# A many-part edit of a two-layer SSM-convolution and MLP training step, with some elementwise products moved to GpSimd

## The chip, the cores and the metric

The kernel runs on one core of a Trainium2 chip. The metric is device time in microseconds: the median of three runs. One further execution was recorded by the hardware profiler, and all rows below come from that one. Engines are named as in the profile: PE is TensorE's matmul, PEld its weight load, DVE is VectorE, ACT is ScalarE, POOL is GpSimd and SP is SyncE. DMAs can be issued from the queues of SP, ACT and POOL.

## The reference

The program is a forward pass of four residual blocks and its full backward pass. Block A is an H3-like layer with a long convolution; block B is an MLP. S is 2048, D is 448, F is 1792, everything in bf16.

```python
def _A_ref(q, k, v, shift_k, ssm_k, ssm_D):
    ...
    for t in range(ks):
        k_shift = k_shift + k_pad[:, t:t + S, :] * shift_k[:, ks - 1 - t][None, None, :]
    kv = k_shift * v
    ...
    y_f = kv_f * kf_f[None, :, :, :]
    y = irfft2(y_f)[:, 0, :S, :]
    y = y + kv * ssm_D[None, None, :]
    return q * y

def _B_ref(x, w1, w2):
    h = _silu(jnp.einsum("bsd,df->bsf", x, w1))
    return jnp.einsum("bsf,fd->bsd", h, w2)

x = A_q
x = x + _A_ref(_layernorm(x, axis=-1), A_k, A_v, A_shift_k, A_ssm_k, A_ssm_D)
x = x + _B_ref(_layernorm(x, axis=-1), B_w1, B_w2)
x = x + _A_ref(_layernorm(x, axis=-1), A_k, A_v, A_shift_k, A_ssm_k, A_ssm_D)
x = x + _B_ref(_layernorm(x, axis=-1), B_w1, B_w2)
return x
```

The outputs are x and the gradients of all inputs but `B_x`. The convolution's result y does not depend on x, so it is computed once and used in both A blocks.

## The kernel before, in words

There are three stages.

**Prefix** (`_ssm_prefix`, 0 to 101 us). The long convolution is done by a two-step Fourier transform on TensorE. For the filter k: its rows are loaded and transposed (L337), a first transform of 16 parts n2 (`_fft_stage1`, L203: two matmuls into a PSUM tile, one copy of 128x896 to SBUF by `_copy`), a turn by seven times 16 transposes (`turn`, L349), and a second transform in 14 blocks of 1024 columns (`_fft_stage2`, L211). `cons_ka` (L397) copies each block of k's spectrum into `Ka`, stores every two blocks to DRAM (`SPEC_d["K"]`, L404), and `_swap_halves_dma` (L241) writes a copy `KB` in which partitions 0 to 63 and 64 to 127 have changed places. All of these DMAs are issued by GpSimd. In the same loop the short convolution of k and the product with v are made (`conv`, L365), and `stage1_kv` (L384) does the first transform of kv, with a copy of 128x448 for each part. `KB` shares its memory with the transposed k and the filter's first rows, so the swaps of blocks 0 to 7 stand after the last convolution (L419). After that loop come the loads of w1 (SP), of the first quarter of grad_out (`gb0`) and of A_q (`x0c0`), both from GpSimd, and the first layernorm of `x0c0` (`_ln`, L253: statistics on VectorE, a power on GpSimd at L270, normalisation on VectorE, a store to `N_d`). Then kv is turned and transformed, and `cons_prod` (L445) does for each of the 14 blocks: copy the block out of PSUM, store kv's spectrum every two blocks, and on VectorE multiply it with `Ka` (L456, `pa`) and with `KB` (L457, `pb`). The inverse transform of a block (`_fft_inv_stage2_chunk`, L222) runs on TensorE two blocks later. The result y goes into `Ysb`.

Copies out of PSUM are given to ScalarE or VectorE by `_Bal` (L87): a running sum of estimated time for each, to which the code adds other work by hand (`bal.add`).

**Main** (`Main.run`, L769, 101 to 510 us). Four chunks of 512 rows go through both layers forward and back. TensorE's order is written out by hand: `H`, `O`, `G`, `N` and `T` are generators of the products with w1, w2, w2 transposed, w1 transposed, and of transposes, and a pattern string gives the order of their steps (`weave`, `steps`). The other engines take their instructions in the order that the scheduler makes of the program. `fwd0(c)` makes the first two layernorms of a chunk and its gate with y, `fwd1(c)` those of the second layer. `O` adds its PSUM result to `X` on VectorE (L685), and in layer 1 stores the finished chunk of `X` to out_0 (L687) when its fourth tile is done. `N` for layer 1 writes the gradient G1 over the same rows of `X` (`Gt`, L723 and `_ln_bwd`, L899). `Main.__init__` stores `Ysb` to `Y_d` from GpSimd (L536).

**Weight gradients and suffix** (`Jobs`, `_ssm_suffix`, 440 us to the end). `Jobs` multiplies stored operands, loaded by SP (L963) as stationary blocks `dstat`, into the gradients of w1 and w2; `fin_w2` (L1051) copies a finished part and stores it from GpSimd. `_ssm_suffix` is the backward pass of the convolution, with the stored spectra loaded by `spec_load` (L1146) and the inverse transform's matrix by `_load_minv` (L199, 1 MB), both from GpSimd. TensorE alternates between the two.

Of the kernel before, what the change touches and what calls it, by code (L numbers as in the profile page):

```python
# [13 lines left out]
ALU = mybir.AluOpType  # L14
# [3 lines left out]
P = 128  # L18
# [184 lines left out]
def _fft_stage1(k, n2, rhs, A1, psum, m=None):  # L203
    nc = k.nc
    ps = psum.tile([P, 2, 512], FP32, name="ps_s1", **k.pt["s1"])
    for c in range(2):
        nc.tensor.matmul(ps[:, c, :D], lhsT=k.M1sb[:, n2 if m is None else m, c, :], rhs=rhs, start=True, stop=True)
    _copy(nc, k.bal.pick(2 * D) if m is None else nc.scalar, A1[:, :, :, n2, :].rearrange("p dh c ds -> p c dh ds"), ps[:, :, :D].rearrange("p c (dh ds) -> p c dh ds", ds=4))
# [44 lines left out]
def _ln(k, pool, c, src, si, n_g, groups=((0, 4),), pin=False, eng=None, behind=None):  # L253
    nc = k.nc
    for lo, hi in groups:
# [3 lines left out]
        for tl in range(lo, hi):  # L259
# [6 lines left out]
            nc.vector.bn_aggr(out=mv[:, tl, :], in_=st[:, tl, :])  # L266
        ve = pool.tile([P, 4], FP32, name="ln_ve", tag="ln_ve", bufs=2)
        nc.vector.tensor_scalar(out=ve[:, 0:n], in0=mv[:, lo:hi, 1], scalar1=EPS, scalar2=None, op0=ALU.add)  # L268
        r = k.rstd[si][:, 4 * c:4 * c + 4]
        nc.gpsimd.tensor_tensor(out=r[:, lo:hi], in0=ve[:, 0:n], in1=k.mhalf[:, 0:n], op=ALU.pow)  # L270
# [7 lines left out]
    if si != 2:  # L278
        lo, hi = groups[0][0], groups[-1][1]
        nc.gpsimd.dma_start(out=_pm(k.N_d[si][:])[:, 4 * c + lo:4 * c + hi, :], in_=n_g[:, lo:hi, :])  # L280


def _ssm_prefix(k):
# [4 lines left out]
    with ExitStack() as es:  # L288
# [35 lines left out]
        for h in range(2):  # L324
            nc.sync.dma_start(out=vn[:, 8 * h:8 * h + 8, :], in_=v_pm[:, 8 * h:8 * h + 8, :])
        _load_minv(k, nc.sync)
        nc.sync.dma_start_transpose(out=k.w2T[:, 0:3, :], in_=k.B_w2[:, 0:384])
        nc.sync.dma_start_transpose(out=k.w2T[:, 3:4, :], in_=k.B_w2[:, 320:448])
# [16 lines left out]
        for n2 in (*range(1, 16), 0):  # L345
            _fft_stage1(k, n2, Kt[:, n2, :], A1K, psum)
# [37 lines left out]
        def stage1_kv(h, jq, kvt):  # L384
            for u in range(0, 4, 2):
# [5 lines left out]
                for w in range(2):  # L391
                    _copy(nc, bal.pick(2 * DH), A1kv[:, 56 * h:56 * (h + 1), :, n2 + w, :].rearrange("p dh c ds -> p c dh ds"),
                          ps[:, w, :, :DH].rearrange("p c (dh ds) -> p c dh ds", ds=4))
# [3 lines left out]
        def cons_ka(ci, ps):  # L397
            sl = slice(ci * 1024, (ci + 1) * 1024)
            _copy(nc, bal.pick(1024), Ka[:, sl], ps[:])
            if ci % 2 == 1:  # L400
                lo, hi = (ci - 1) * 1024, (ci + 1) * 1024
                if ci > 8:
                    _swap_halves_dma(k, KB, Ka, lo, hi, nc.gpsimd)
                nc.gpsimd.dma_start(out=k.SPEC_d["K"][:, lo:hi], in_=Ka[:, lo:hi])  # L404

        prev = None
        for h in range(2):
            for i, jq in enumerate((1, 2, 3, 0)):
# [8 lines left out]
                else:  # L417
                    _fft_stage2(k, Z, psum, cons_ka, range(2 * i, 2 * i + 2))
        for i in range(4):  # L419
            _swap_halves_dma(k, KB, Ka, 2048 * i, 2048 * (i + 1), nc.gpsimd)  # L420
# [8 lines left out]
        k.gb0 = _hd(k, [P, 4, D], "gb0")  # L429
        nc.gpsimd.dma_start(out=k.gb0[:], in_=_pm(k.grad_out[0])[:, 0:4, :])  # L430
        k.x0c0 = _hd(k, [P, 4, D], "x0c0")
        nc.gpsimd.dma_start(out=k.x0c0[:], in_=_pm(k.A_q[0])[:, 0:4, :])
        k.na0 = _hd(k, [P, 4, D], "na0")
        _ln(k, work, 0, lambda tl: k.x0c0[:, tl, :], 0, k.na0, pin=True)


# [8 lines left out]
        def cons_prod(ci, ps):  # L445
# [11 lines left out]
            nc.vector.tensor_tensor(out=pb[:], in0=xs, in1=KB[:, sl], op=ALU.mult)  # L457
            bal.add("dve", 1.4)
# [65 lines left out]
class Main:  # L524
    def __init__(self, k, es):
# [10 lines left out]
        nc.gpsimd.dma_start(out=_pm(k.Y_d[:]), in_=k.Ysb[:])  # L536
# [61 lines left out]
    def a_fwd(self, c, si, src, n_g, groups, behind=None):  # L598
        nc, X = self.nc, self.X
        if len(groups) > 2:  # L600

            for g in groups:
                _ln(self.k, self.ch, c, src, si, n_g, (g,))
                self.gate(c, src, n_g, (g,))
            return
# [18 lines left out]
    def fwd0(self, c):  # L624
# [14 lines left out]
        n01 = self.t([P, 4, D], "n01", bufs=2)  # L639
        _ln(k, self.ch, c, self.xs(c), 1, n01)  # L640
        self.n0[c] = (n00, n01)

    def fwd1(self, c, behind=None):
        n10, n11 = self.t([P, 4, D], "n10"), self.t([P, 4, D], "n11")
        pairs = ((0, 2), (2, 4)) if c else ((0, 2), (2, 3), (3, 4))
        self.a_fwd(c, 2, self.xs(c), n10, pairs, behind)
        _ln(self.k, self.ch, c, self.xs(c), 3, n11, pairs)
# [28 lines left out]
    def O(self, c, L, aT):  # L676
        nc, k, X = self.nc, self.k, self.X
        for tl in range(4):
# [7 lines left out]
            if L == 1 and tl == 3:  # L686
                nc.gpsimd.dma_start(out=_pm(k.outs[0][0])[:, 4 * c:4 * c + 4, :], in_=X[:, 4 * c:4 * c + 4, :])  # L687
# [26 lines left out]
    def N(self, c, L, gh, gres, n_b, n_a):  # L714
# [4 lines left out]
        for tl in range(4):  # L719
# [3 lines left out]
            Gt = self.X[:, t, :] if L == 1 else g1[:, tl % 2, :]  # L723
            pn = k.psum.tile([P, 512], FP32, name="ps_n", tag="po", bufs=2)
# [6 lines left out]
            _ln_bwd(k, self.ch, u0[:], n_b[:, tl, :], cp[:, tl, :], gres(tl), Gt)  # L731
            if L == 1:
                nc.vector.tensor_tensor(out=gyt[:, tl, :], in0=Gt, in1=n_a[:, tl, :], op=ALU.mult)
                u1 = self.t([P, D], "lb_u1", "lb_u0", 3)
                nc.vector.scalar_tensor_tensor(out=u1[:], in0=Gt, scalar=k.rstd[2][:, t:t + 1], in1=self.Y[:, t, :], op0=ALU.mult, op1=ALU.mult, accum_out=cp[:, 4 + tl, 0:1])
                self.chain = _ln_bwd(k, self.ch, u1[:], n_a[:, tl, :], cp[:, 4 + tl, :], Gt, Gt)
# [32 lines left out]
    def run(self, es):  # L769
# [19 lines left out]
        with tc.high_priority():  # L789
            self.fwd0(0)  # L790
        nT = self.nT()
# [7 lines left out]
        steps("GGGtttt", G=g20, t=self.T2(self.n0[0][1], nT))  # L799
# [20 lines left out]
        for c in range(4):  # L820
# [6 lines left out]
            o = self.O(c, 1, aT2)  # L827
            if c == 0:
                weave("O" * 8, O=o)
            else:  # L830
# [5 lines left out]
                if c == 1:  # L836
                    weave("OOOOOGGOGGOTOT", O=o, G=g, T=self.T(self.n0[c + 1][1], nT))
# [492 lines left out]
```

## Time and profile before

| | us |
|---|---|
| median of 3 runs (725.36 to 734.2) | 729.11 |
| the profiled execution | 729.0 |
| its span, first to last instruction | 727.2 |
| TensorE matmul busy | 685.5 (94%) |
| VectorE busy | 489.0 (67%) |
| ScalarE busy | 444.3 (61%) |
| GpSimd busy | 126.4 (17%) |

The span is what the rows below can explain; 1.8 us lie around it. Busy shares are means over stages with different limits. A matmul's recorded time holds its pipeline, so TensorE can look busy where it is fed slowly. In the groups and the timeline a row reads: line, engine, operation, output and inputs, shapes, count; the bracket at its end gives the idle time of that engine just before the row and what ended it. The granted clock is the share of full clock that TensorE was given. Rows of the timeline that are merged have a count above one.

### The profile page before, as it was taken

What the parts mean: (1) busy time and instruction counts of PE and PEld (TensorE: products, weight loads), DVE (VectorE), ACT (ScalarE), POOL (GpSimd) and SP (SyncE); (2) the same over time, 40 slices, a digit from 0 to 9 for tenths busy, and PEclk for the clock granted to TensorE, in tenths of its full rate; (3) what the DMA queues carried; (4) which work ended last, traced back from release to release, by engine and by line L of the source; (5) the groups of instructions that cost most, each with busy time, mean ns of one, the idle gap of its engine ahead of it and who ended that gap; (6) DMA issues with size and microseconds to landing.
All of it is one profiled execution on the core that took longest, in us unless ns stands there. A gap on an engine that the chain in (4) does not pass through costs nothing.

```text
span 727.2 us, 12726 instructions
## 1 busy us (share of the span) xinstructions
PE 685.5 (94%) x4933; PEld 377.5 (52%) x4976; DVE 489.0 (67%) x1157; ACT 444.3 (61%) x585; POOL 126.4 (17%) x213
## 2 busy tenths in 40 slices
PE   5997889998989999999999999999899999999996
PEld 4986644434444444444444444545466666656553
DVE  4789865656897747976379534825168768859760
ACT  4887877686777868779687783132755555454200
POOL 1134410201011100111001000000312323244220
PEclk9999999999999999999999999999999999999999
DMA  9949799899989999499985997199998798789860
GB/s 315 292 141 289 249 298 135 126 264 248 211 202 243 220 240 242 109 228 262 186 200 130 244 244 299 30 222 218 369 411 298 251 337 288 244 307 357 314 210 20
DMA packets 195581, 172.59 MB, mean 237 GB/s; under 512 B 142882, under 2 KB 173730, under 8 KB 194368
## 3 DMA queue, kind: packets, MB, share of 16 engines
q1 hardware_dynamic: 180992, 115.73, 63.1%
q0 software_dynamic: 14064, 56.04, 22.2%
q8 instruction: 39, 0.64, 0.4%
q14 instruction: 22, 0.18, 0.1%
q10 hardware_dynamic: 464, 0.00, 0.0%
HBM read 73.25 MB, written 60.10 MB: 183 GB/s over the span
## 4 chain that ended last, share of the span: by engine, by line
PE 59%; issue 10%; DVE 6%; DMA 3%; ACT 3%; POOL 2%; SPq 1%; POOLq 0%; DVEq 0%
PE ps_d L969 12%; PE ps_g L499 10%; PE ps_n L726 10%; PE ps_h L499 9%; PE ps_o L681 8%; PE ps_d L1004 2%; DMA dstat<-a_d 2%; PE ps_v L228 2%; PE ps_v L227 2%; PE ps_t L567 1%; DMA out_dram<-X 1%; DVE B1v L1276 1%; PE ps_tr L1158 1%; ACT dT L674 1%; DVE gka L1277 1%
## 5 line engine op out<-in xcount | busy, mean ns | idle before, releaser
L969 PEld LDWEIGHTS <-dstat 128*128 128x128 bf16 x800 | 75.5, 98 | 69.0 <-DMA dstat<-a_d 4.0
L499 PE MATMUL ps_h<-nT,w1sb 128*128 128x512 bf16 (+1 forms) x434 | 95.9, 380 | 5.6 <-ACT dT L664 2.2
L681 PE MATMUL ps_o<-w2sb,aT 128*128 128x448 bf16 x448 | 88.8, 352 | 4.0 <-DVE X L685 4.0
L726 PE MATMUL ps_n<-w1T,ghT 128*128 128x448 bf16 x448 | 92.1, 352 | 0.1
L499 PE MATMUL ps_g<-nT,w2T 128*128 128x512 bf16 (+1 forms) x378 | 81.1, 380 | 1.1 <-issue 0.5
L709 ACT CAST ghT<-ps_g 128x512 bf16<-128x512 f32 (+1 forms) x74 | 54.1, 761 | 42.4 <-PE ps_g L499 42.2
L659 ACT ACTIVATE aT<-ps_h 128x512 bf16<-128x512 f32 (+1 forms) x82 | 59.9, 758 | 29.9 <-PE ps_h L499 27.4
L499 PEld LDWEIGHTS <-w1sb 128*128 128x128 bf16 (+1 forms) x448 | 35.5, 97 | 61.7 <-issue 27.7
L681 PEld LDWEIGHTS <-aT 128*128 128x128 bf16 x448 | 43.5, 98 | 44.5 <-issue 4.5
L726 PEld LDWEIGHTS <-ghT 128*128 128x128 bf16 x448 | 43.3, 98 | 41.0 <-DVE ghT L711 1.4
L499 PEld LDWEIGHTS <-w2T 128*128 128x128 bf16 (+1 forms) x448 | 35.3, 97 | 55.3 <-issue 20.9
L894 DVE SCALAR_TENSOR_TENSOR lb_v<-lb_u,n 128x448 bf16<-128x448 bf16 x48 | 29.9, 623 | 42.9 <-ACT lb_u L730 42.4
L270 POOL TENSOR_TENSOR rstd<-ln_ve,mhalf 128x2 f32<-128x2 f32 (+2 forms) x27 | 23.8, 881 | 193.7 <-DVE ln_ve L268 193.7
L674 ACT ACTIVATE dT<-dT 128x1024 bf16<-128x1024 bf16 (+1 forms) x64 | 55.0, 937 | 0.1
L969 PE MATMUL ps_d<-n3m,dstat 128*128 128x448 bf16 x224 | 48.6, 352 | 0.2
L969 PE MATMUL ps_d<-n1m,dstat 128*128 128x448 bf16 x224 | 48.6, 352 | 0.1
L227 PE MATMUL ps_v<-Gsb,pa 128*128 128x128 bf16 x336 | 44.2, 223 | 2.7 <-DVE pa L456 2.6
L228 PE MATMUL ps_v<-Gsb,pb 128*128 128x128 bf16 x336 | 43.5, 223 | 1.9 <-DVE pb L457 1.9
L664 ACT CAST dT<-ps_h 128x1024 bf16<-128x1024 f32 (+1 forms) x50 | 42.7, 871 | 0.0
L730 ACT ACTIVATE lb_u<-ps_n,rstd 128x448 bf16<-128x448 f32 x32 | 20.7, 647 | 33.2 <-PE ps_n L726 25.4
L969 PE MATMUL ps_d<-go,dstat 128*128 128x448 bf16 x176 | 37.2, 353 | 2.7 <-DMA dstat<-a_d 1.5
L969 PE MATMUL ps_d<-X,dstat 128*128 128x448 bf16 x176 | 37.1, 353 | 1.6 <-DMA dstat<-a_d 1.6
(209 smaller groups left out, 1188.7 us busy)
## 6 DMA issues: line engine op xcount, KB each, us to landing
dstat<-g_d SPq DMA_DIRECT2D x28, 512.0 KB, 5.7
dstat<-a_d SPq DMA_DIRECT2D x26, 512.0 KB, 6.0
a_d<-turned SPq DMA_DIRECT2D x16, 512.0 KB, 3.6
g_d<-turned SPq DMA_DIRECT2D x16, 512.0 KB, 3.3
a_d<-turned SPq DMA_DIRECT2D x16, 384.0 KB, 3.0
g_d<-turned SPq DMA_DIRECT2D x16, 384.0 KB, 3.3
N_d<-n POOLq DMA_DIRECT2D x10, 448.0 KB, 4.1
spec_K<-Z POOLq DMA_DIRECT2D x7, 512.0 KB, 7.1
```

The source lines that it names most:

```text
L227: nc.tensor.matmul(pv[:, i, :], lhsT=pa[:, i * P:(i + 1) * P], rhs=k.Gsb[:, ga, :], start=True, stop=False)
L228: nc.tensor.matmul(pv[:, i, :], lhsT=pb[:, i * P:(i + 1) * P], rhs=k.Gsb[:, gb, :], start=False, stop=True)
L270: nc.gpsimd.tensor_tensor(out=r[:, lo:hi], in0=ve[:, 0:n], in1=k.mhalf[:, 0:n], op=ALU.pow)
L499: nc.tensor.matmul(ps(u, u + 1)[:, 0, :], lhsT=wT[h, b, ft * P:(ft + 1) * P], rhs=rhs[h, b, :], start=start, stop=stop)
L659: self.last_silu = nc.scalar.activation(aT[hh][:, o:o + hi - lo, :], ps(lo, hi), ACT.Silu)
L664: nc.scalar.copy(self.dpart(dT, 2 * fp + lo, 2 * fp + hi), ps(lo, hi))
L674: self.nc.scalar.activation(d[:, o:o + n, :], d[:, o:o + n, :], ACT.Derivative_silu)
L681: nc.tensor.matmul(po[:, :D], lhsT=aT[ft // 7][:, ft % 7, tl * P:(tl + 1) * P], rhs=self.w2sb[:, ft, :], start=(ft == 0), stop=(ft == NF - 1))
L709: nc.scalar.copy(g, ps(lo, hi))
L726: nc.tensor.matmul(pn[:, :D], lhsT=gh[ft // 7][:, ft % 7, tl * P:(tl + 1) * P], rhs=self.w1T[:, ft, :], start=(ft == 0), stop=(ft == NF - 1))
L894: nc.vector.scalar_tensor_tensor(out=v[:], in0=u0, scalar=-1.0 / D, in1=n_t, op0=ALU.mult, op1=ALU.mult, accum_out=cp[:, 1:2])
L969: self.nc.tensor.matmul(ps[:, :D], lhsT=st[:, t, :], rhs=mov[:, t, :], start=(first and t == 0), stop=(last and t == NT - 1))
```

## The change

It has these parts. (1) The first transform of k gives its copies to VectorE and ScalarE in turn. (2) `stage1_kv` copies two parts at once. (3) `x0c0` is loaded by SP behind v, `gb0` by SP behind w2's transposed loads; the first layernorm becomes a generator (`_ln_steps`) whose statistics are spread over the second half of the convolution loop. (4) The swaps into `KB` and the stores of k's spectrum are issued by SP. (5) `pb` of blocks 1, 4, 7, 10 and 13 is computed by GpSimd. (6) The store of `Ysb` is put behind the power of the second layernorm. (7) The first steps of `Main` go G, G, three transposes, G. (8) `fwd1(0)` finishes each group of tiles through both layernorms before the next. (9) The second layernorm of `fwd0` becomes `fwd0b`, called after the first two tiles of `O`. (10) out_0 is stored in pairs of tiles, and G1 of layer 1 has a tile of its own (`gmid`). (11) The last copy of w2's gradient is split over ScalarE and VectorE, and the last two stores go from SP. (12) In the suffix the inverse matrix is loaded behind the third pair of spectrum loads.

```diff
-def _fft_stage1(k, n2, rhs, A1, psum, m=None):
+def _fft_stage1(k, n2, rhs, A1, psum, m=None, eng=None):
...
-    _copy(nc, k.bal.pick(2 * D) if m is None else nc.scalar, A1[:, :, :, n2, :].rearrange("p dh c ds -> p c dh ds"), ps[:, :, :D].rearrange("p c (dh ds) -> p c dh ds", ds=4))
+    _copy(nc, eng or nc.scalar, A1[:, :, :, n2, :].rearrange("p dh c ds -> p c dh ds"), ps[:, :, :D].rearrange("p c (dh ds) -> p c dh ds", ds=4))
...
-def _ln(k, pool, c, src, si, n_g, groups=((0, 4),), pin=False, eng=None, behind=None):
+def _ln_steps(k, pool, c, src, si, n_g, groups=((0, 4),), pin=False, eng=None, behind=None, store=()):
...
             nc.vector.bn_aggr(out=mv[:, tl, :], in_=st[:, tl, :])
+            yield
...
-        nc.gpsimd.tensor_tensor(out=r[:, lo:hi], in0=ve[:, 0:n], in1=k.mhalf[:, 0:n], op=ALU.pow)
+        k.ln_pow = nc.gpsimd.tensor_tensor(out=r[:, lo:hi], in0=ve[:, 0:n], in1=k.mhalf[:, 0:n], op=ALU.pow)
...
+def _ln(*args, **kw):
+    for _ in _ln_steps(*args, **kw):
+        pass
...
+        k.x0c0 = _hd(k, [P, 4, D], "x0c0")
+        nc.sync.dma_start(out=k.x0c0[:], in_=_pm(k.A_q[0])[:, 0:4, :])
         _load_minv(k, nc.sync)
...
+        for i, n2 in enumerate((*range(1, 16), 0)):
+            _fft_stage1(k, n2, Kt[:, n2, :], A1K, psum, eng=nc.vector if i % 2 and i != 9 else nc.scalar)
+        bal.reset()
...
-                for w in range(2):
-                    _copy(nc, bal.pick(2 * DH), A1kv[:, 56 * h:56 * (h + 1), :, n2 + w, :].rearrange("p dh c ds -> p c dh ds"),
-                          ps[:, w, :, :DH].rearrange("p c (dh ds) -> p c dh ds", ds=4))
+                _copy(nc, bal.pick(4 * DH), A1kv[:, 56 * h:56 * (h + 1), :, n2:n2 + 2, :].rearrange("p dh c n ds -> p c dh n ds"),
+                      ps[:, :, :, :DH].rearrange("p n c (dh ds) -> p c dh n ds", ds=4))
...
-                    _swap_halves_dma(k, KB, Ka, lo, hi, nc.gpsimd)
-                nc.gpsimd.dma_start(out=k.SPEC_d["K"][:, lo:hi], in_=Ka[:, lo:hi])
+                    _swap_halves_dma(k, KB, Ka, lo, hi, nc.sync)
+                nc.sync.dma_start(out=k.SPEC_d["K"][:, lo:hi], in_=Ka[:, lo:hi])
+
+        k.gb0 = _hd(k, [P, 4, D], "gb0")
+        with tc.issue_after(w2.ins):
+            nc.sync.dma_start(out=k.gb0[:], in_=_pm(k.grad_out[0])[:, 0:4, :])
+        k.na0 = _hd(k, [P, 4, D], "na0")
+        ln0 = _ln_steps(k, work, 0, lambda tl: k.x0c0[:, tl, :], 0, k.na0, pin=True)
...
                     _fft_stage2(k, Z, psum, cons_ka, range(2 * i, 2 * i + 2))
+                    next(ln0, None)
+        for _ in ln0:
+            pass
         for i in range(4):
-            _swap_halves_dma(k, KB, Ka, 2048 * i, 2048 * (i + 1), nc.gpsimd)
+            _swap_halves_dma(k, KB, Ka, 2048 * i, 2048 * (i + 1), nc.sync)
...
-            nc.vector.tensor_tensor(out=pb[:], in0=xs, in1=KB[:, sl], op=ALU.mult)
-            bal.add("dve", 1.4)
+            (nc.gpsimd if ci % 3 == 1 else nc.vector).tensor_tensor(out=pb[:], in0=xs, in1=KB[:, sl], op=ALU.mult)
+            bal.add("dve", 0.7 if ci % 3 == 1 else 1.4)
...
-        nc.gpsimd.dma_start(out=_pm(k.Y_d[:]), in_=k.Ysb[:])
...
+    def fwd0b(self, c):
+        _ln(self.k, self.ch, c, self.xs(c), 1, self.n0[c][1])
...
+            for g in pairs:
+                _ln(self.k, self.ch, c, self.xs(c), 2, n10, (g,))
+                self.gate(c, self.xs(c), n10, (g,))
+                _ln(self.k, self.ch, c, self.xs(c), 3, n11, (g,), store=(0, 4) if g[1] == 4 else None)
...
-            if L == 1 and tl == 3:
-                nc.gpsimd.dma_start(out=_pm(k.outs[0][0])[:, 4 * c:4 * c + 4, :], in_=X[:, 4 * c:4 * c + 4, :])
+            if L == 1 and tl % 2:
+                nc.gpsimd.dma_start(out=_pm(k.outs[0][0])[:, t - 1:t + 1, :], in_=X[:, t - 1:t + 1, :])
...
+            G1 = self.t([P, D], "gmid")[:] if L == 1 else Gt
...
-            _ln_bwd(k, self.ch, u0[:], n_b[:, tl, :], cp[:, tl, :], gres(tl), Gt)
+            _ln_bwd(k, self.ch, u0[:], n_b[:, tl, :], cp[:, tl, :], gres(tl), G1)
...
-                self.chain = _ln_bwd(k, self.ch, u1[:], n_a[:, tl, :], cp[:, 4 + tl, :], Gt, Gt)
+                self.chain = _ln_bwd(k, self.ch, u1[:], n_a[:, tl, :], cp[:, 4 + tl, :], G1, Gt)
...
+        with tc.issue_after(k.ln_pow.ins):
+            nc.gpsimd.dma_start(out=_pm(k.Y_d[:]), in_=k.Ysb[:])
...
-        steps("GGGtttt", G=g20, t=self.T2(self.n0[0][1], nT))
+        steps("GGtttG", G=g20, t=self.T2(self.n0[0][1], nT))
...
             o = self.O(c, 1, aT2)
+            steps("OOOO", O=o)
+            if c < 3:
+                self.fwd0b(c + 1)
...
-        nc.scalar.copy(o[:], ps[:, :D])
+        if ft == NF - 1:
+            nc.scalar.copy(o[:, 0:256], ps[:, 0:256])
+            nc.vector.tensor_copy(o[:, 256:D], ps[:, 256:D])
+        else:
+            nc.scalar.copy(o[:], ps[:, :D])
         self.flush()
-        nc.gpsimd.dma_start(out=k.outs[8][ft * P:(ft + 1) * P, :], in_=o[:])
+        (nc.gpsimd if ft < NF - 2 else nc.sync).dma_start(out=k.outs[8][ft * P:(ft + 1) * P, :], in_=o[:])
...
-        _load_minv(k, nc.gpsimd)
...
+                if cp == 2:
+                    with tc.issue_after(i.ins):
+                        _load_minv(k, nc.gpsimd)
```

## The prediction

> **What bounds the kernel now.** I read the page first, then TensorE's waits, its timeline for the place of every gap over 0.1 us, and then the timelines of the engine that ended each gap.
>
> ```profile
> span 727.2 us, 12726 instructions
> ...
> PE 685.5 (94%) x4933; PEld 377.5 (52%) x4976; DVE 489.0 (67%) x1157; ACT 444.3 (61%) x585; POOL 126.4 (17%) x213
> ```
>
> TensorE is idle for 41.7 us of the span, and no other engine is near full on average. The change removes no matmul, so its gain lies in those gaps, in stretches where TensorE only looks busy, and in the tail. TensorE's waits name them (total, times, longest):
>
> ```profile
> PE ps_o L681 <- DVE X L685: 4.0, 2, 2.1
> PE ps_d L969 <- DMA dstat<-a_d: 3.2, 2, 1.6
> PE ps_v L227 <- DVE pa L456: 2.6, 4, 1.3
> ...
> PE ps_v L228 <- DVE pb L457: 1.9, 4, 1.2
> PE ps_h L499 <- ACT nT L766: 1.6, 1, 1.6
> ...
> PE ps_t L765 <- DVE n L277: 1.2, 1, 1.2
> ```
>
> Between 64 and 95 us (k times kv, the product stage) VectorE is full in most slices. The stretches (PE, PEld, DVE, ACT, POOL, then granted clock) show TensorE at half clock after a near-idle 4 us:
>
> ```profile
> 66.00:68.00 2.00, 0.71 (x3) 0.10 (x1) 2.00 (x4) 2.00 (x3) 0.52 (x1) 1.00 1.06 244
> 68.00:70.00 2.00, 0.81 (x7) 0.39 (x8) 2.00 (x5) 1.07 (x2) 0.57 (x1) 1.00 1.07 246
> 70.00:72.00 2.00, 2.00 (x20) 1.73 (x18) 2.00 (x4) 1.47 (x2) 1.04 (x2) 0.50 1.01 236
> 72.00:74.00 2.00, 2.00 (x24) 1.88 (x22) 1.34 (x3) 0.88 (x2) 1.09 (x2) 0.64 1.00 272
> ```
>
> VectorE's timeline holds two stalls that matter (the bracket is the idle time before the row and what ended it):
>
> ```profile
> 75.52 0.69 DVE L456 TENSOR_TENSOR pa<-A1K,Z 128x1024 bf16<-128x1024 bf16 x1 [2.18 <-ACT A1K L111]
> ...
> 183.85 0.39 DVE L899 TENSOR_TENSOR X<-lb_v,gb 128x448 bf16<-128x448 bf16 x1 [5.18 <-DMA out_dram<-X]
> ```
>
> GpSimd's timeline shows how its two-input operation fares beside VectorE, and when the last store goes out:
>
> ```profile
> 158.67 1.04 POOL L270 TENSOR_TENSOR rstd<-ln_ve,mhalf 128x4 f32<-128x4 f32 x1 [15.32 <-DVE ln_ve L268]
> ...
> 168.19 1.94 POOL L270 TENSOR_TENSOR rstd<-ln_ve,mhalf 128x4 f32<-128x4 f32 x1 [5.45 <-DVE ln_ve L268]
> ...
> 724.01 0.54 POOL L1056 DMA_DIRECT2D out_dram<-dout  x1 [7.41 <-issue]
> ```
>
> The same power takes 1.04 us while VectorE stands, and 1.94 us where it meets VectorE's two-input product of 168.01 to 169.23: it waited the product out.
>
> **The sum** is made against the profiled execution: 729.0 us, of which 727.2 are span; the median of the three runs is 729.11, so both scales agree.
>
> *Start (L207).* Sixteen copies of 0.83 (ScalarE) or 1.0 us (VectorE) follow from 13.5 us; ScalarE has 10 of them and the last ends at 22.7. Nine and seven take 9 x 0.83 = 7.5 us, to about 21. M1's second half, awaited until 17.3, should land 1 to 2 us sooner: the 0.9 MB of gb0 and x0c0 were on GpSimd's queue from 5.1 and 10.7 and shared 410 GB/s with it; now one stands behind v, the other behind w2T. I take -1.7 (0 if M1 lands no sooner and the transposes that follow wait, -2.0 at best).
>
> *Convolution (25 to 57).* TensorE is full here (18.1 of 19 us), so merged stage-1 copies (32 of 0.53/0.62 become 16 of 0.83/1.0) only free ScalarE and VectorE. The layernorm's statistics, 4 x (0.6 + 0.17) us, come in: VectorE's 3.07 us of a 3.40 us period falls by some 0.4 and gains 0.76, about even with TensorE. +0.3 (0 to +1).
>
> *Product stage.* From the first pa (68.43) to the last pb (93.07) VectorE needs 24.6 us: 28 products at a pitch of 0.60, three copies of 1.14, the normalisation 1.35, and 2.7 idle, of which 2.18 follow the half clock. The statistics leave the stretch before, where copies and statistics keep VectorE full until 68.4; TensorE's transposes end at 65.15, and product 0 needs 0.4 of matmul and 1.0 of copy: it starts at 66.5, -1.9. The normalisation goes too (its 0.55 us store on GpSimd with it), as does the idle time, if the near-idle 4 us go. Then 23 products stay on VectorE: 13.8 us. The balancer, told 0.7 in place of 1.4 for five blocks, gives VectorE about 6 copies: 6.8 us. For a product on GpSimd no row has a like: its memsets of 1344 and 256 elements (1.24 and 0.33 us) give 0.84 ns an element for one pass and 0.1 fixed, so two reads and a write are two to three passes, 1.8 to 2.7 us; I take 2.3, 2.2 of it in memory. Does VectorE stand meanwhile? The pair of powers shows GpSimd waiting for VectorE; a power of 4 elements is too short to show the reverse. Bounds: VectorE loses nothing, or 2.2 us each time. I take the loss, since the row has the two engines exclude each other. Port time is then 13.8 + 5 x 2.2 = 24.8; of the copies, which read PSUM, I let half lie beside (no row tells): 24.8 + 3.4 = 28.2 against 24.6, +3.6, and with the earlier start +1.7. Bounds: -3.5 (1.8 each, all copies hidden) to +7.6 (2.7, none hidden). On GpSimd's own queue the products stand before the stores of kv's spectrum (0.54 each, seven), which wait behind them for at most 2.3 us with nothing due soon; TensorE waits for a product two blocks after it starts, some 3 us, so one of 2.3 us is covered, save block 13's, whose wait ends the port's sum anyway.
> The Trainium skill (SBUF — State Buffer, Who interferes with whom) has the rule behind this: a VectorE instruction with two SBUF inputs and a GpSimd instruction that reads SBUF lock each other out for a whole instruction; the 1.94 against 1.04 us agree for the one direction. Its GPSIMD Engine Reference (3.1) has 4497 ns for 2048 fp32, so 2.25 us for 1024 would be an estimate by that page; the sum by it would be the same to 0.3 us.
>
> *Swaps and spectrum stores to SyncE.* 21 transfers leave GpSimd (11.2 us of issue at 0.52 to 0.56, with waits of up to 2.8), where the power stood behind them until 75.55 though its input was ready at 68.5. SP's queue is free from 34 to 53 us and pays 0.4 to 0.6 each. They now share one queue with w1's 1.6 MB; at 245 to 285 GB/s that is 6 us, and the first swaps, issued from 54, have until 67. 0.
>
> *From y to H (97 to 110).* The store of Y held the powers from 101.1 to 103.64; they now go first. n is ready near 104 in place of 106.4, two G steps fill TensorE until 105.7, the transposes follow, and the third G covers most of ScalarE's 2.0 us of copies before H. Of the 1.63 us gap, -1.0 (0 to -1.6).
>
> *fwd1(0).* The first pair's normalisation follows its own gate in place of standing behind three groups: the 1.21 us gap at 139.6 goes. The later transposes sit between G steps. -1.2 (0 to -1.2).
>
> *O and fwd0b.* The gap of 2.13 at 167.5 is an X addition queued behind the second layernorm's statistics; it moves ahead of them. VectorE is nearly full from 156 to 176, so the products at L845 are late next: -1.3 (0 to -2.1). In later blocks no gap stands here: 0.
>
> *gmid and paired stores.* VectorE's 5.18 us stall on the out_0 store, which landed at 183.8, made it late until the gap of 1.90 at 203.3. G1 no longer touches X, and the final write comes after stores issued near 165: -1.9 (-1 to -1.9). Two more stores cost GpSimd 0.54 each, unseen.
>
> *Minv later (516).* Its 1 MB shares some 410 GB/s with the dstat load awaited for 1.63 us at 527; but the next spectrum load, held by Minv for 5.5 us, moves up into its place. -0.8 (0 to -1.6). Later GpSimd has 4 to 7 us between issues, and TensorE shows no gap there.
>
> *Tail.* ScalarE ends at 721.82; GpSimd issues at 724.01 and ends the span 3.2 later. SP has had no load since 703: issue near 721.8, and 0.2 from splitting the copy; some of the 2.2 may be a wait that any queue has. -2.2 (-0.3 to -2.7).
>
> Sum: -1.7 + 0.3 + 1.7 - 1.0 - 1.2 - 1.3 - 1.9 - 0.8 - 2.2 = -8.1: 720.9 us.
>
> **Rivals.**
> *GpSimd free beside VectorE.* For it: no VectorE product in the trace is longer than 0.69 beside a power (75.55). The stage takes 13.8 + 6.8 = 20.6, and block 13's product ends 1.0 later than on VectorE: 20.6 + 1.0 - 24.6 - 1.9 = -4.9 in place of +1.7. 714.3 us.
> *Swaps late.* w1 and the stores go ahead of the swaps in SP's one queue; pb(0) stands beyond 67. Against: w1 alone leaves 5 us of slack. If half of the spectrum stores (1.8 MB, 7 us) come ahead as well as w1 (6) and the first two blocks' swap takes 2, it lands at 54 + 15 = 69, two late, and the stall brings back the half clock's 2.2 us: +4.2, 725.1 us.
> *Slower: the product on GpSimd far dearer.* Place: the five blocks. Each us of hold costs 5. With half the copies hidden, the change loses from a hold of 2.2 + 8.1 / 5 = 3.8 us; at 5 us it ends at 735. For it: the longest power took 1.94 for 4 elements, so GpSimd can be held off long by a stream of VectorE products, and TensorE, two blocks ahead, would stand and fall to half clock again. Against: the memsets.
>
> **How the numbers follow.** Likeliest, 0.55: 720.9, by itself 716 to 726. GpSimd free 0.27, late swaps 0.08, dear product 0.10. A run of this kernel tells about 1% (7.3 us) from no change: the marks are 721.8 and 736.4. Faster: 0.33 of the likeliest and all of the free case, 0.60. Slower: half of the dear case, 0.05. The rest 0.35. The range leaves a tenth on each side: 712.5 reaches past the free case, 727 past late swaps.
>
> **What would show it.** Right: products (pa, pb) on VectorE of 2 us or more, or gaps beside each GpSimd product of 2.3 us; no wait of ps_t L765 on n, of ps_o on X, or of L899 on the out_0 store; last copy to end of span below 4 us. Wrong: unhindered products beside GpSimd (then 714), a GpSimd product over 3.8 us (then no gain), VectorE waiting for KB's swap, or H starting after 110 us (108.9 by the sum).

## The result and the profile after

| kernel | median us | ratio to before, 95% interval |
|---|---|---|
| before, beside it | 729.38 (20 runs) | 1 |
| changed | 733.10 (20 runs, 728.35 to 741.36) | 1.0046 [1.0028, 1.0064] |
| changed, on another chip (after_again) | 737.36, before 731.51 | 1.0063 [1.0034, 1.0093] |

The forecast was 720.9 us. The change does not gain; it loses about half a per cent, less than the 1% mark but above zero in both intervals. The first profile of the changed kernel is its fastest execution of the twenty (728.35), so a second one, after_again, stands beside it below.

The first lines of the changed kernel's page, span and busy time:

```profile
span 726.5 us, 12762 instructions
...
PE 691.2 (95%) x4976; PEld 378.7 (52%) x4976; DVE 496.2 (68%) x1147; ACT 439.7 (61%) x575; POOL 126.1 (17%) x197
```

The shares hardly move, GpSimd's neither: what it lost in DMA issues it got in products. TensorE's waits (total, times, longest):

```profile
PE ps_v L227 <- DVE pa L467: 6.7, 6, 1.6
...
PE ps_d L986 <- DMA dstat<-a_d: 2.4, 2, 1.2
PE ps_t L777 <- DVE n L278: 1.9, 1, 1.9
...
PE ps_sk L1288 <- issue: 1.4, 1, 1.4
...
PE ps_v L228 <- POOL pb L468: 1.3, 1, 1.3
...
PE ps_h L510 <- ACT nT L778: 0.5, 1, 0.5
```

The waits of ps_o on X (4.0 us) are gone, and the one at ps_h fell from 1.6 to 0.5. In their place the product stage has grown: 6.7 us on pa where there were 2.6, and 1.3 on GpSimd's pb. VectorE's timeline in that stage, changed kernel:

```profile
72.98 0.69 DVE L467 TENSOR_TENSOR pa<-A1K,Z 128x1024 bf16<-128x1024 bf16 x1
75.22 0.98 DVE L467 TENSOR_TENSOR pa<-A1K,Z 128x1024 bf16<-128x1024 bf16 x1 [1.55 <-ACT A1K L111]
...
79.01 0.69 DVE L468 TENSOR_TENSOR pb<-A1K,KB 128x1024 bf16<-128x1024 bf16 x1
79.61 2.65 DVE L467 TENSOR_TENSOR pa<-A1K,Z 128x1024 bf16<-128x1024 bf16 x1
...
93.90 1.23 DVE L113 COPY X<-ps_t 128x2048 bf16<-128x2048 bf16 x1
```

And GpSimd's timeline over the same time:

```profile
73.18 2.48 POOL L468 TENSOR_TENSOR pb<-A1K,KB 128x1024 bf16<-128x1024 bf16 x1 [2.86 <-DMA spec_K<-Z]
...
79.58 2.13 POOL L468 TENSOR_TENSOR pb<-A1K,KB 128x1024 bf16<-128x1024 bf16 x1
...
93.91 2.13 POOL L468 TENSOR_TENSOR pb<-A1K,KB 128x1024 bf16<-128x1024 bf16 x1
```

Read the two side by side. GpSimd's product runs from 79.58 to 81.71; the VectorE product issued at 79.61 takes 2.65 us where its neighbour takes 0.69, so it ran only behind GpSimd's. The same happens at 84.53, with 2.69 us. At 73.18 it is the other way round: VectorE's product of 72.98 came first, and GpSimd's took 2.48 in place of 2.13. The copy at 93.90, which reads PSUM, takes 1.23 beside a GpSimd product, as a copy of this shape does alone (1.22 in no_gp below).

The stretches (PE, PEld, DVE, ACT, POOL, then granted clock, DMA share, GB/s) of the changed kernel show half clock three times up to 110 us, where the kernel before showed it once:

```profile
72.00:74.00 2.00, 2.00 (x16) 1.44 (x14) 1.64 (x2) 1.75 (x2) 0.82 (x1) 0.50 1.02 395
...
90.00:92.00 2.00, 2.00 (x16) 1.45 (x14) 1.92 (x4) 1.79 (x3) 0.44 (x1) 0.50 0.51 207
...
100.00:102.00 2.00, 2.00 (x7) 0.85 (x6) 1.57 (x2) 0.65 (x1) 0.00 (x0) 0.50 1.10 339
```

The first two spells lie inside the product stage, the third behind it, on the last matmuls of the inverse transform (`ps_y`). What the third costs can be read from their 32 matmuls, in the changed kernel and then in no_gp (an experiment below), where no half clock falls on them:

```profile
98.52 7.90 PE L493 MATMUL ps_y<-A1kv,Minvsb 128*128 128x448 bf16 x32 [1.41 <-DVE A1kv L113]
```

```profile
93.64 6.23 PE L493 MATMUL ps_y<-A1kv,Minvsb 128*128 128x448 bf16 x32 [1.10 <-ACT A1kv L111]
```

The same work takes 1.67 us longer. It takes 6.23 us in both profiles of before, too, and 7.51 in after_again, where half clock lies from 101.35 to 104.77.

The tail is as forecast here: the last store leaves from SyncE's queue right behind the last copy, and the span ends 3.7 us after TensorE's last matmul where it was 6.0.

**Where the time went**, cut at places that all kernels have. Each entry is the length of the part minus its length in the kernel before: the first measured column against the first profile of before, the others against a second one (before_again, span 729.6 us). best_again is the version kept in the end, without a product on GpSimd (below).

| part | forecast | changed, first profile | after_again | best_again |
|---|---|---|---|---|
| up to the first pa | -3.3 | -2.9 | -0.8 | -1.1 |
| first pa to end of last pb | +3.6 | +5.8 | +6.8 | -1.9 |
| to H's first wait | -1.0 | +0.8 | +0.6 | -1.0 |
| to the next block's H (241) | -4.4 | -2.8 | -0.9 | -2.8 |
| to the end of the MLP blocks (475) | 0 | 0.0 | 0.0 | -0.1 |
| to the second wait for dstat (527) | -0.8 | -0.8 | +2.2 | +0.7 |
| to ps_sk (676) | 0 | +1.4 | +1.2 | +1.8 |
| to the end | -2.2 | -2.3 | -0.7 | -2.3 |
| span | -8.1 | -0.7 | +8.3 | -6.7 |

The two profiles of the changed kernel lie on either side of a usual run: their mean is +3.8 us, and the medians differ by 3.7. Against the forecast the mean misses 11.9 us: 2.7 in the product stage, 1.7 from there to H, 2.6 to the next block's H, 1.5 up to the first pa, and 3.5 behind 475 us.

### The profile page after: what moved, and what is told of

Same layout as the page of the kernel before. It is cut to its first block, busy times and chain, and to the rows that moved or that the text cites. A ratio compares the mean times of both kernels' runs of the same rounds, so it can differ in the third digit from the quotient of the medians.

```text
span 726.5 us, 12762 instructions
## 1 busy us (share of the span) xinstructions
PE 691.2 (95%) x4976; PEld 378.7 (52%) x4976; DVE 496.2 (68%) x1147; ACT 439.7 (61%) x575; POOL 126.1 (17%) x197
## 4 chain that ended last, share of the span: by engine, by line
PE 71%; DMA 3%; issue 3%; DVE 3%; ACT 3%; POOL 1%; POOLq 0%; ACTq 0%
PE ps_d L986 19%; PE ps_n L738 12%; PE ps_h L510 11%; PE ps_g L510 10%; PE ps_o L692 8%; PE ps_d L1021 2%; DMA dstat<-a_d 2%; PE ps_v L228 2%; PE ps_v L227 2%; DMA go<-in_grad_out_dram 2%; PE ps_t L577 1%; PE ps_tr L1181 1%; PE ps_gkv L1255 1%; PE ps_s L1198 1%; ACT dT L685 1%
## 5 line engine op out<-in xcount | busy, mean ns | idle before, releaser
L510 PE MATMUL ps_h<-nT,w1sb 128*128 128x512 bf16 (+1 forms) x448 | 97.4, 380 | 2.6 <-ACT dT L675 1.9
L510 PE MATMUL ps_g<-nT,w2T 128*128 128x512 bf16 (+1 forms) x392 | 82.8, 380 | 0.1
L738 PEld LDWEIGHTS <-ghT 128*128 128x128 bf16 x448 | 43.2, 98 | 42.2 <-DVE ghT L862 1.4
L271 POOL TENSOR_TENSOR rstd<-ln_ve,mhalf 128x2 f32<-128x2 f32 (+2 forms) x27 | 22.3, 827 | 200.8 <-DVE ln_ve L269 200.8
L227 PEld LDWEIGHTS <-pa 128*128 128x128 bf16 x336 | 34.0, 101 | 12.1 <-DVE pa L467 8.7
```

Source lines behind the costliest of these rows:

```text
L227: nc.tensor.matmul(pv[:, i, :], lhsT=pa[:, i * P:(i + 1) * P], rhs=k.Gsb[:, ga, :], start=True, stop=False)
L271: k.ln_pow = nc.gpsimd.tensor_tensor(out=r[:, lo:hi], in0=ve[:, 0:n], in1=k.mhalf[:, 0:n], op=ALU.pow)
L510: nc.tensor.matmul(ps(u, u + 1)[:, 0, :], lhsT=wT[h, b, ft * P:(ft + 1) * P], rhs=rhs[h, b, :], start=start, stop=stop)
L738: nc.tensor.matmul(pn[:, :D], lhsT=gh[ft // 7][:, ft % 7, tl * P:(tl + 1) * P], rhs=self.w1T[:, ft, :], start=(ft == 0), stop=(ft == NF - 1))
```

## The experiments

Ratios are against the kernel before on the same chip. Theory at the start: the product on GpSimd shuts VectorE out, and the rest of the change gains. Rival: GpSimd's product is about neutral, and the gains forecast elsewhere failed.

**no_gp**: the changed kernel with all products on VectorE.

```
-            (nc.gpsimd if ci % 3 == 1 else nc.vector).tensor_tensor(out=pb[:], in0=xs, in1=KB[:, sl], op=ALU.mult)
-            bal.add("dve", 0.7 if ci % 3 == 1 else 1.4)
+            nc.vector.tensor_tensor(out=pb[:], in0=xs, in1=KB[:, sl], op=ALU.mult)
+            bal.add("dve", 1.4)
```

> The changed kernel with all 14 products by KB on VectorE again (and 1.4 told to the balancer). Theory (lock-out): the product stage falls from 30.5 us (first pa to last pb) to 22 to 24, no pa is longer than 0.7 us, H starts near 105 to 107 in place of 113.4; median 723 to 726 us, 7 to 10 under the changed kernel. Rival (the product on GpSimd is about neutral, and the loss is in other parts): within 2 us of the changed kernel, 731 to 735.

Measured: 724.84 us, 0.9898 [0.9847, 0.9949], 12.5 us under after_again on the same chip. Its first products (min/median/max ns, first and last start):

```profile
L467 DVE TENSOR_TENSOR pa<-A1K,Z x14: 681/685/691, 70.2 to 90.2; 128x1024 bf16<-128x1024 bf16 x14
```

The same row of the changed kernel:

```profile
L467 DVE TENSOR_TENSOR pa<-A1K,Z x14: 676/692/2694, 65.6 to 93.1; 128x1024 bf16<-128x1024 bf16 x14
```

None is shut out in no_gp, and the stage takes 21.3 us, in which VectorE stands for 0.66. The rival falls: the five products on GpSimd cost 12.5 us by the medians, more than the 7 to 10 expected. Part of that goes with half clock. The mean span of the runs is 11.1 us longer with them, and the clock not granted (its share times the span, a mean over the runs) comes to 6.6 us in after_again and 2.7 in no_gp, so half clock accounts for 3.9 of the 11.1 at most.

**after_again**: the changed kernel once more, without an edit.

> The changed kernel unaltered, for a second profile: the recorded one (728.4 us) was the fastest of its 20 executions, 4.7 us under their median. Theory (half clock): a typical execution has TensorE at half clock for longer between 65 and 110 us than the recorded one (about 10 us there), and H starts later than its 113.4 us, by 2 to 5 us. Rival (waits on DMA): the extra time lies after 440 us, in waits for the weight gradients' operands, with H at 113 to 114 us. Median 731 to 735 us by both.

Measured: 737.36 us, 1.0063 [1.0034, 1.0093]. The stage took 30.0 us with no half clock inside it, against 30.5 with two spells of it in the first profile: half clock is not what makes the stage long. H started at 116.68, 3.3 us later than in the first profile, but the first pa was already 4.1 us later (69.64 against 65.57). The median lies above the 731 to 735 expected, on a chip where before is slower as well. The waits behind 480 us were longer, as the rival had it:

```profile
PE ps_d L986 <- DMA dstat<-a_d: 5.5, 2, 3.4
...
PE ps_sk L1288 <- DMA out_dram<-B1v: 2.8, 1, 2.8
```

**before_gp**: the kernel before, with the product line of the diff alone.

```
-            nc.vector.tensor_tensor(out=pb[:], in0=xs, in1=KB[:, sl], op=ALU.mult)
-            bal.add("dve", 1.4)
+            (nc.gpsimd if ci % 3 == 1 else nc.vector).tensor_tensor(out=pb[:], in0=xs, in1=KB[:, sl], op=ALU.mult)
+            bal.add("dve", 0.7 if ci % 3 == 1 else 1.4)
```

> The kernel before with only the product by KB of every third block on GpSimd. Theory (lock-out): five pa of 2.6 us, 5 to 8 us slower than before: 734 to 738 us. Rival (neutral): 728 to 731 us.

Measured: 745.95 us, 1.0191 [1.0152, 1.0231]: +14.4 us, dearer than expected. The stage took 38.3 us. Here swaps and stores are still on GpSimd's own queue, and the first product stands behind them until 80.35, eleven us after the first pa; TensorE runs at half clock from 75.18 to 85.42 and from 95.66 to 102.49. So the 14.4 us are not the price of the lock-out alone. GpSimd's timeline in before_gp:

```profile
79.79 0.55 POOL L280 DMA_DIRECT2D N_d<-na  x1 [1.30 <-DVE na L277]
80.35 2.31 POOL L457 TENSOR_TENSOR pb<-A1K,KB 128x1024 bf16<-128x1024 bf16 x1
```

**no_gp_swpool**: no_gp with the half swaps and k's spectrum stores issued from GpSimd again.

```
-                    _swap_halves_dma(k, KB, Ka, lo, hi, nc.sync)
-                nc.sync.dma_start(out=k.SPEC_d["K"][:, lo:hi], in_=Ka[:, lo:hi])
+                    _swap_halves_dma(k, KB, Ka, lo, hi, nc.gpsimd)
+                nc.gpsimd.dma_start(out=k.SPEC_d["K"][:, lo:hi], in_=Ka[:, lo:hi])
...
-            _swap_halves_dma(k, KB, Ka, 2048 * i, 2048 * (i + 1), nc.sync)
+            _swap_halves_dma(k, KB, Ka, 2048 * i, 2048 * (i + 1), nc.gpsimd)
```

> The changed kernel with all products on VectorE and with the swaps and k's spectrum stores on GpSimd's queue again. Theory (lock-out alone makes the loss): within 2 us of the same kernel with the swaps on SyncE. Rival (one queue for swaps, stores and w1 makes them late): 3 us or more faster than that kernel. Second rival (GpSimd's waits between swaps hold up later work): 3 us or more slower.

Measured: 728.15 us, 0.9930 [0.9898, 0.9962], 3.3 us over no_gp, with intervals that overlap. One wait in its trace can be pointed at, VectorE's for the first swap:

```profile
71.15 0.69 DVE L468 TENSOR_TENSOR pb<-A1K,KB 128x1024 bf16<-128x1024 bf16 x1 [1.04 <-DMA KB<-Z]
```

So the swaps on SyncE are worth 1.0 us by the trace; the times are too close to say more, and do not decide between the expectation and its second rival.

**gp_psum**: the changed kernel, with both VectorE products of the block behind each GpSimd block reading the spectrum from PSUM in fp32, so that these blocks are rounded once less.

```
+            xv = ps[:] if ci % 3 == 2 else xs
-            nc.vector.tensor_tensor(out=pa[:], in0=xs, in1=Ka[:, sl], op=ALU.mult)
+            nc.vector.tensor_tensor(out=pa[:], in0=xv, in1=Ka[:, sl], op=ALU.mult)
-            (nc.gpsimd if ci % 3 == 1 else nc.vector).tensor_tensor(out=pb[:], in0=xs, in1=KB[:, sl], op=ALU.mult)
+            (nc.gpsimd if ci % 3 == 1 else nc.vector).tensor_tensor(out=pb[:], in0=xv if ci % 3 == 2 else xs, in1=KB[:, sl], op=ALU.mult)
```

> The changed kernel, but in the blocks after a GpSimd block both VectorE products read the spectrum from PSUM in fp32 rather than its bf16 copy in SBUF. Theory (a VectorE instruction with two bf16 inputs from SBUF and GpSimd's product shut each other out): none of these products waits the GpSimd product out; each takes 1.1 to 1.3 us, its plain time with a PSUM input, instead of 0.69 free and 2.65 shut out, and the pair is some 0.9 us shorter per block; the GpSimd product stays at 2.1 to 2.5. The kernel is 2 to 5 us faster than the changed kernel, still slower than no_gp. Rival (both engines share SBUF bandwidth, or wait for GpSimd's data by dependence): pa of these blocks still takes over 2 us, and the GpSimd product over 3.

Measured: 730.18 us, 0.9991 [0.9957, 1.0025], 4 to 5 us better than the changed kernel by the ratios. The trace places about 2 of them: from the first pa to H it is 45.4 us, against 47.9 and 47.0 in the two profiles of the changed kernel. VectorE in gp_psum:

```profile
69.90 1.22 DVE L468 TENSOR_TENSOR pa<-ps_s,Z 128x1024 bf16<-128x1024 f32 x1
71.04 1.21 DVE L469 TENSOR_TENSOR pb<-ps_s,KB 128x1024 bf16<-128x1024 f32 x1
...
86.42 2.61 DVE L468 TENSOR_TENSOR pa<-A1K,Z 128x1024 bf16<-128x1024 bf16 x1
...
92.94 2.92 DVE L469 TENSOR_TENSOR pb<-A1K,KB 128x1024 bf16<-128x1024 bf16 x1
```

GpSimd in gp_psum:

```profile
69.81 2.13 POOL L469 TENSOR_TENSOR pb<-A1K,KB 128x1024 bf16<-128x1024 bf16 x1
...
86.30 2.18 POOL L469 TENSOR_TENSOR pb<-A1K,KB 128x1024 bf16<-128x1024 bf16 x1
...
93.18 2.13 POOL L469 TENSOR_TENSOR pb<-A1K,KB 128x1024 bf16<-128x1024 bf16 x1
```

From 69.90 to 71.94 both engines multiply and neither is slowed: with one input from PSUM these products are not locked out. In the same run the products with two SBUF inputs that meet GpSimd's (86.42 and 92.94) still take 2.61 and 2.92. A shared bandwidth would have stretched both; that rival falls. The Trainium skill (SBUF — State Buffer, Who interferes with whom) has a VectorE instruction with at most one SBUF input not contend with GpSimd, one with two contend, and the order of issue decide who waits; 1.22, 2.61 and the 2.48 above agree with the three. One row does not fit the third: the VectorE product recorded from 92.94 waited although GpSimd's is recorded only from 93.18, so the recorded starts do not always tell who goes first.

**gp_no13**: the changed kernel with block 13's product on VectorE.

```
-            (nc.gpsimd if ci % 3 == 1 else nc.vector).tensor_tensor(out=pb[:], in0=xs, in1=KB[:, sl], op=ALU.mult)
-            bal.add("dve", 0.7 if ci % 3 == 1 else 1.4)
+            (nc.gpsimd if ci % 3 == 1 and ci < 13 else nc.vector).tensor_tensor(out=pb[:], in0=xs, in1=KB[:, sl], op=ALU.mult)
+            bal.add("dve", 0.7 if ci % 3 == 1 and ci < 13 else 1.4)
```

> The changed kernel with block 13's second product on VectorE, so that four of fourteen are on GpSimd and the last, which has nothing behind it, is not. Theory: the uncovered wait of 1.28 us at the end and the thin stretch behind it go, with the half clock at ps_y: 2 to 4 us faster than the changed kernel, that is still 0 to 3 us slower than the kernel before. Rival: the cost lies in the four shut-out products in the middle alone, and this is within 1 us of the changed kernel.

Measured: 728.07 us, 0.9977 [0.9942, 1.0012], 5 to 6 us better than the changed kernel by the ratios, more than the 2 to 4 expected, and by its interval not to be told from before. The last product, which has nothing behind it, was the dearest: from the first pa to H it is 43.2 us here, against 47.0 and 47.9 with all five and 36.8 in no_gp, so about 4 us for the last and 1.6 for each of the other four. Of the 4, about 2 are in the stage and the rest behind it, where `ps_y` took 6.23 us again, without half clock. The stage took 28.4 us with no half clock in it at all, still 7.1 more than without GpSimd, 1.8 for each of four products.

**no_gp_minv**: no_gp with the Minv load at its old place.

```
             jobs.run(1)
+        _load_minv(k, nc.gpsimd)
...
-                if cp == 2:
-                    with tc.issue_after(i.ins):
-                        _load_minv(k, nc.gpsimd)
```

> All products on VectorE, and Minv loaded again straight after the last part's first-stage loop, as in the kernel before. Theory: in the kernel before, that load stands in GpSimd's queue and waits about 5 us for the store of g (idle 4.84 us before it in the profile of before_gp), and with it wait the four 512 KB loads of the spectra behind it; moved away, those loads start at once and take bandwidth from the statistics' loads, so that the two waits on dstat grew from 1.69 and 1.54 us to 1.85 and 3.48, and the late Minv makes the wait at ps_sk 4.05 us instead of 0.48. So the move, forecast at -0.8, costs 2 at dstat and 3.5 at ps_sk: this kernel takes 3 to 6 us less than no_gp (about 0.982 to 0.986 of before), with waits of about 1.6, 1.5 and 0.4 us. Rival: the longer waits belong to this chip's slower transfers or to the paired stores, and the move is worth its -0.8: this kernel is as fast as no_gp or up to 1 us slower, with waits on dstat above 3 us still.

Measured: 722.62 us, 0.9869 [0.9823, 0.9915]; the waits on dstat were 2.37 and 1.97, and ps_sk showed none. That is 0.3% better than no_gp, between what the theory and the rival expected; the two ran on different chips and the intervals overlap, so it decides nothing.

**no_gp_minv_fwd**: the same, and the old order in fwd1(0).

```
             for g in pairs:
                 _ln(self.k, self.ch, c, self.xs(c), 2, n10, (g,))
                 self.gate(c, self.xs(c), n10, (g,))
-                _ln(self.k, self.ch, c, self.xs(c), 3, n11, (g,), store=(0, 4) if g[1] == 4 else None)
+            _ln(self.k, self.ch, c, self.xs(c), 3, n11, pairs)
```

> no_gp_minv with the first block's second normalization in the old order (all three groups first, then the other layer's). Theory: the new order puts each group's chain behind its own wait for the power on GpSimd, and the wait at ps_t is 1.92 us where it was 1.21; the old order brings 0.6 to 1.0 us, too little to be sure of in times (0.998 to 1.0 of no_gp_minv), but the gap at ps_t reads 1.2 in the trace. Rival (the forecast of the change): the old order is 1.2 us dearer.

Measured: 720.80 us, 0.9848 [0.9807, 0.9890]; the wait at ps_t went from 1.92 to 1.19 us, and the part from H to the next block's H is 0.4 shorter than in no_gp. The last four runs shared a chip.

**no_gp_fwd**: no_gp with the old fwd1(0) alone, so that only Minv's place tells it from best_again, which is no_gp_minv_fwd once more.

> No product on GpSimd, the first block's second normalization in the old order, and Minv late as in the change; on the same chip as best_again, from which only the place of the Minv load differs. Theory (the load at its old place held the spectra's loads back behind the store of g, and late it lets them in before the statistics): the waits at dstat and ps_sk add up to 7 to 10 us in this profile against 3.5 to 5 in best_again, and it is 2 to 5 us slower than best_again. Since gp_no13 and gp_psum, with the load late, showed sums of only 2.7 and 3.5 us, the rival is strong: the sums vary from execution to execution for another reason, and the two kernels are within 1 us of each other.

> The same kernel as no_gp_minv_fwd: no product on GpSimd, the Minv load and the first block's second normalization as before. It should give 0.981 to 0.989 of before again, about 719 to 722 us where before takes 730, if the ranking of the versions holds on another chip; a ratio above 0.992 would mean that the chip made it.

Measured: no_gp_fwd 723.37 us, 0.9909 [0.9872, 0.9945]; best_again 723.19, 0.9869 [0.9830, 0.9908]. The medians are alike and the intervals overlap. The queue does behave as the theory has it. GpSimd in best_again, Minv early:

```profile
507.86 0.54 POOL L200 DMA_DIRECT2D Minvs<-c_minv  x1 [3.55 <-PE ps_s L207]
...
519.09 0.53 POOL L1171 DMA_DIRECT2D kk_d<-spec_K  x1 [6.97 <-DMA Minvs<-c_minv]
```

In no_gp, Minv late:

```profile
507.97 0.53 POOL L1170 DMA_DIRECT2D kk_c<-spec_K  x1 [0.26 <-PE ps_s L207]
...
509.66 0.53 POOL L1170 DMA_DIRECT2D kk_d<-spec_K  x1
```

The loads of kk_d start nine us earlier, into the time of the statistics' loads. But the sum of the waits at dstat and ps_sk does not follow that alone: with Minv late it was 8.2, 9.4 and 10.0 us in three profiles of one chip and 2.7, 3.5, 3.8 and 6.0 in four others; with Minv early 3.6 to 5.7 in seven. On the chip of the 8.2 to 10.0 the one early profile (before_gp) had 3.7; on that of the 2.7 and 3.5 the two early ones had 4.3 and 5.0, so there it is the other way round. Whether the move costs or gains anything stays open; no measured time shows a gain.

**best_old_s1**: best_again, with the copies of k's first stage dealt out as before.

```
-    _copy(nc, eng or nc.scalar, A1[:, :, :, n2, :].rearrange("p dh c ds -> p c dh ds"), ...)
+    _copy(nc, k.bal.pick(2 * D) if m is None else nc.scalar, A1[:, :, :, n2, :].rearrange("p dh c ds -> p c dh ds"), ...)
...
-        for i, n2 in enumerate((*range(1, 16), 0)):
-            _fft_stage1(k, n2, Kt[:, n2, :], A1K, psum, eng=nc.vector if i % 2 and i != 9 else nc.scalar)
-        bal.reset()
+        for n2 in (*range(1, 16), 0):
+            _fft_stage1(k, n2, Kt[:, n2, :], A1K, psum)
```

> best_again with the copies of k's first stage dealt out by the balance as in the kernel before, not in turn to VectorE and ScalarE. Forecast of the change: the turn saves 1.7 us, so this is 1.7 us slower. Theory from the traces: where the stage's matmuls run at 0.58 us instead of 0.35 (all profiles but the first two), TensorE sets this stage's pace and the turn saves 0 to 0.8 us from the first of these matmuls to the first transpose of kT (8.4 and 9.0 us in the two old forms, 9.3 to 9.7 in six of seven new ones), so the times agree within 1 us.

Measured: 723.14 us, 0.9874 [0.9835, 0.9913]: equal to best_again. From the first of these matmuls to the first transpose of kT it is 8.75 us here and 8.73 in best_again.

**before_again**: the kernel before, for its profile.

> The kernel before itself, for a second profile. If the slow first matmuls belong to the chip and not to the change, they show 0.58 us here too, the first product starts at 68 to 70 us, and the product stage lasts 24 to 25 us again; the waits at dstat and ps_sk add up to 3 to 5 us.

Measured: 731.34 us, span 729.6. The stage took 23.2 us. The first matmuls are slow here too. TensorE's timeline in before_again:

```profile
14.24 4.84 PE L207 MATMUL ps_s<-Z,M1sb 128*128 128x448 bf16 x14 [0.99 <-ACT Z L111]
...
23.28 0.89 PE L360 MATMUL ps_kT<-ident,Ysb 128*112 128x128 bf16 x13
```

And in best_again:

```profile
14.63 4.16 PE L207 MATMUL ps_s<-Z,M1sb 128*128 128x448 bf16 x14 [0.99 <-ACT Z L111]
...
23.36 0.83 PE L369 MATMUL ps_kT<-ident,Ysb 128*112 128x128 bf16 x12
```

The first matmuls of these rows start 373 ns apart, the later ones of the stage 188 where nothing holds them. While they are slow TensorE sets the pace of this stage, and how the copies are dealt out hardly matters: kT's transposes begin at 23.28 in the one and 23.36 in the other, and best_old_s1 above is the direct test.

## Why the prediction was wrong, by its steps

*Product stage* (+3.6 forecast, +5.8 and +6.8 measured): this is the step that failed, together with what follows it up to H. Its mechanism held: lock-out, also in the direction that no row of before showed, by a GpSimd product of 2.13 us (2.3 taken). Its sum did not. The forecast's 28.2 us were 13.8 of products + 11.0 of lock-out + 3.4 of copies. In the first profile the 30.5 are 13.8 of products, 6.2 of lock-out (the excess of the long products), 5.9 for five copies, 2.9 of VectorE standing, mostly for ScalarE's copies, 0.9 for the last GpSimd product behind VectorE's end, and 0.8 of small gaps. The lock-out with the last product came to 7.1 in place of 11.0, since two of the five products met VectorE idle (73.7 to 75.2) or in a copy from PSUM (93.90). The copies were taken 2.5 us too short, half of them being let lie beside GpSimd. VectorE's standing (2.9) and the small gaps (0.8) were put at nothing, since TensorE, two blocks ahead, was taken to be covered. So errors of both signs partly cancel, and that the stage came within 2 to 3 us of its forecast is in part luck.

Behind the stage the sum had no term for what a late and thin end of it does. From its end to H the forecast was -1.0 and +0.8 and +0.6 came; the 1.7 and 1.3 us that half clock added to `ps_y` are nearly all of that miss. Whether a spell falls there is not settled by GpSimd alone: gp_psum, with all five products, has 6.23 us for `ps_y`, and best_old_s1, with none, has 7.91.

The change was also a poor one by the prediction's own terms, which did not say so. The stage was set against the 24.6 us of before, which held 2.7 of idle time and 1.35 of normalisation that other parts of the change remove by themselves. Without GpSimd those terms give 28 products at 0.60 and three copies of 1.14, some 20.2 us, so they put the products on GpSimd at 8.0 us; no_gp took 21.3 (with 0.66 idle), and they cost 8.7 in the stage and 12.0 in the span (after_again less no_gp). Of the other 3.3, 1.6 lie between the stage and H, and 1.5 in the part after H. That last is no price of GpSimd: after_again has a spell of half clock there, from 152.6 to 156.0, and no_gp_minv, which has one from 140.6 to 144.1, takes as long.

*Rivals.* GpSimd free beside VectorE: fell with the products of 2.65 us. Swaps late: VectorE waited for no swap. Dear product: the time came near its 735, but the hold never passed 2.1 us in the changed kernel. Half clock came back, as that rival said, yet after_again and gp_no13 have long stages without it. Of the signs of being wrong, H after 110 us came: 113.42 and 116.68.

*Up to the first pa* (-3.3, of which the start -1.7): -2.9 in the first profile, where kT's transposes moved from 21.27 to 19.60. That it hits the 1.7 is in part luck: 0.8 of it is there before the stage's first matmul (12.91 and 12.11 us). Where the first matmuls are slow, the start's share is 0 and -0.8 to -1.1 remains.

*From y to H* (-1.0): exact without GpSimd, and lost with it, as above. *O, gmid and paired stores* (-3.2): right; the waits on ps_o and on the out_0 store went, and 0.49 us at L862 came, the products that the text had named to be late next. *fwd1(0)* (-1.2): wrong. Each group's chain now runs behind its own wait for GpSimd's power, where the other groups' statistics filled those waits before; the gap grew from 1.21 to 1.92 and stands behind the last group. *Minv* (-0.8): between nothing and a loss, as above. *Tail* (-2.2): -2.3, but only -0.7 in after_again, where ScalarE stood 7.3 us for an earlier store and half clock lay from 688 to 692.

Outside the product stage the forecast parts come to -11.7, or -9.7 without the two that best_again undoes; it has -4.8 there. What is missing is the start where the first matmuls are slow (2.2) and 2.5 us after 475 us. Of those, waits for transfers show only 0.4 (dstat +0.7, grad_out +0.5, ps_sk -0.8 against before_again); waits for VectorE's pb in the suffix (L1210) are 1.1 longer and one for ScalarE 0.4; the rest stays open.

## What to carry to other kernels

When a change has several parts, price the doubtful part against the kernel that has all the others: idle time that they remove is no longer there to be filled. A VectorE product with two bf16 inputs in SBUF does not run beside GpSimd's, so moving it trades 0.6 us of VectorE for up to 2 of waiting. It costs less where the VectorE work beside it reads PSUM, but in no run here does it pay. The last product of the stage was the dearest one to move (about 4 us, against 1.6 for each of the others), since no work was left to cover it. Of the versions here best_again, without the product on GpSimd and with fwd1(0) and Minv as before, is the one to keep: 0.9848 [0.9807, 0.9890] of before on one chip and 0.9869 [0.9830, 0.9908] on another. The times do not tell it from the other versions without that product whose Minv or fwd1(0) differ.

## What the runs showed of the hardware

The lock-out goes by operands: a VectorE product of this shape took 1.22 us beside GpSimd's with one input in PSUM, 2.60 to 2.69 with both in SBUF where it met the whole of it (once 2.92), and 0.69 alone.

A slow TensorE need not show in the granted clock. In twelve of fourteen profiles the first 8 to 15 of the 128x448 matmuls took up to 0.58 us (0.35 later) and started 373 ns apart in place of 188, half the rate, for 3 to 6 us, while the clock column read 1.00; the two others are the first profiles of either kernel. The trace's list of clock changes tells why the column is silent: it has no entry for the time before its first, which is a full clock at 18.41 us in before_again and 17.40 in best_again, within 0.3 us of the end of the last slow matmul, but at 11.99 and 10.17 in the two first profiles, before the stage begins. The Trainium skill (TensorE: Matmul & The Clock Gate, Part 1) has the first few us of matmuls at half rate, for a time that varies from run to run; these traces agree, though 64 smaller matmuls, with gaps, had run before.

A spell of half clock has a price where TensorE sets the pace: it lasts 3.41 us, and the 32 matmuls of `ps_y` took 7.90 and 7.51 us with one beside 6.23 without. In the product stage, where VectorE is the fuller engine, 30.5 us with two spells and 30.0 with none show no such price.
